# Feed-forward gradients: du and dg of tiles 2 to 14 transposed by DMA, products two tiles behind

## The chip, the cores and the metric

The kernel runs on one core of a Trainium2 chip. The metric is the device time of the whole program, in microseconds. A core has a matrix engine (PE, with its weight loads shown as PEld), a vector engine (DVE), a scalar engine (ACT), GpSimd (POOL) and a queue engine (SP, its DMA issues shown as SPq). 16 DMA engines move data between HBM and the on-chip memory SBUF. Matrix results land in PSUM, which has banks of 128 x 512 f32.

## What is computed

The reference runs a four-layer network forward and then takes the gradients of its input and of all its weights. Layers 0 and 2 are linear attention, layers 1 and 3 are a gated feed-forward block; two sets of weights are shared by the layers of a kind.

```python
def _B_ref(x, w_gate, w_up, w_down):
    g = jnp.einsum("bsd,df->bsf", x, w_gate)
    u = jnp.einsum("bsd,df->bsf", x, w_up)
    h = _sigmoid(g) * u
    return jnp.einsum("bsf,fd->bsd", h, w_down)

x = A_x
x = x + _A_ref(_layernorm(x, axis=-1), A_wqkv, A_wo)
x = x + _B_ref(_layernorm(x, axis=-1), B_w_gate, B_w_up, B_w_down)
x = x + _A_ref(_layernorm(x, axis=-1), A_wqkv, A_wo)
x = x + _B_ref(_layernorm(x, axis=-1), B_w_gate, B_w_up, B_w_down)
...
_out, _vjp = jax.vjp(_f, A_x, A_wqkv, A_wo, B_w_gate, B_w_up, B_w_down)
_grads = _vjp(grad_out)
```

There are S = 2048 rows, D = 512 model columns and F = 1376 feed-forward columns, all bf16 outside. For a feed-forward layer with incoming gradient G the backward pass needs dh = G w_down^T, then du = dh * sigmoid(g) and dg = dh * u * sigmoid(g) * (1 - sigmoid(g)), then the gradient of the normalised input, du w_up^T + dg w_gate^T, the layer norm's own backward step, and the weight gradients, which are products over all rows.

## The kernel before

The rows are 16 tiles of 128 (NST = 16). F is cut into NFC = 11 chunks of 128, the last of 96 columns, and into three slices of 512, 512 and 352 (FSL). The program runs forward through the four layers, then backward through layers 3, 2, 1 and 0. The backward pass of a feed-forward layer is `b_bwd_p1`, called once for layer 3 and once for layer 1; its weight gradients are computed later, from what it stores, in between the next layers' work (`p2_gen`).

The order of instructions on PE, ACT, DVE and POOL is the order in which the code is written (`tc.manual_schedule`). DMA issues, all of them on SP in this kernel, are ordered by a scheduler. A tile of a pool has as many buffers as `bufs` says; an instruction that writes a tile again waits until all that read the old contents in that buffer have ended.

For a tile st, `b_bwd_p1` does this:

- `load`: `ssd`, the two saved factors for du and dg (128 x 2 x 1376, L1101), is loaded from HBM one tile ahead, two buffers; `h_ld` (L1027) comes for two tiles at a time.
- `dhh_mm` (L1004): for each of the three slices, 4 matmuls of `gT` (the transposed gradient tile) with `wdT` into a bank of `dhh_ps`, of which there are two.
- `dd_ops` (L1012): two DVE multiplications for each slice make `dd[:, 0]` (du) and `dd[:, 1]` (dg), bf16. `dd` has two buffers; in layer 3 (`first`) the even tiles use one in the pool `pre` (`pre_dd`), the odd ones another.
- `transposes` (L1079 on PE, L1081 and L1083 on ACT): 22 transposes for each tile, 8, 8 and 6 of them for the three slices, through PSUM (`T_ps`), copied by ACT into `ddT`.
- `store` (L1124, L1126): three DMAs write `dd` to HBM, in pieces of 256 columns (512 bytes) and of 96 columns.
- `dh_mm` (L1113): 22 matmuls of `ddT` with `wuT` and `wgT` into the one bank of `dh_ps`, for the tile before (st-1), in pieces of 11, 5 and 6 between the other work.
- `ln_begin` (`t_sb`, L970 on ACT), `sums` (L975) and `add` (L982, L983) on DVE: the layer norm's backward step, one tile later still.
- `g_tile` and `gT_make`: the incoming gradient of tile st+2 is loaded (layer 3, L1058) or cast and stored (layer 1, L1061 and L1063), and that of st+1 is transposed by 4 PE transposes (L996) and an ACT copy (L997).

So PE's order in iteration st is: 8 matmuls of `dhh` (slices 0 and 1), 11 products of tile st-1, 8 transposes, 4 matmuls of `dhh` (slice 2), 4 transposes of g, 5 products, 8 transposes, 6 products, 6 transposes. After the loop come the 22 products of tile 15.

In layer 3, `mid` loads the eight operand blocks (512 KB each) of the coming weight gradients (`b_operands`, issued at L1202, tiles `p_a`), all after the load of `ssd` for tile 8. In layer 1 the operands are loaded as their buffers come free.

Of the kernel before, what the change touches and what calls it, by code (L numbers as in the profile page):

```python
# [9 lines left out]
BF16 = mybir.dt.bfloat16  # L10
# [8 lines left out]
D = 512  # L19
# [5 lines left out]
NDC = D // P  # L25
NFC = (F + P - 1) // P
FLAST = F - (NFC - 1) * P
FSL = [(0, 512), (512, 512), (1024, F - 1024)]
EPS_LN = 1e-5
EPS = 1e-6  # L30
# [30 lines left out]
def kernel(  # L61
# [78 lines left out]
    with tc.tile_pool(name="wfwd", bufs=1, reuse_waits="tile") as wfwd, ExitStack() as lctx, tc.manual_schedule(engines=EM):  # L140
# [51 lines left out]
        with tc.tile_pool(name="aq2", bufs=1, reuse_waits="tile") as aq:  # L192
            A = kq_fwd(k, aq, 2, lns[2], lns[3])
            hctx.close()
            wb = bctx.enter_context(tc.tile_pool(name="wbwd", bufs=1, side="right", reuse_waits="tile"))
            ocur = {}
            prectx = ExitStack()
            pre = prectx.enter_context(tc.tile_pool(name="pre", bufs=1, side="right", reuse_waits="tile"))
            k.pre = {"pool": pre}

            def out_cb(st):
                if st == NB:
                    k.pre["g"] = pre.tile([P, 2, D], BF16, name="pre_g")
                    nc.sync.dma_start(out=k.pre["g"][:], in_=dram_batch(g_in, 0, 2))
                    k.pre["ssd"] = pre.tile([P, 2, F], BF16, name="pre_ssd")
                    nc.sync.dma_start(out=k.pre["ssd"][:], in_=k.sv[3]["ssd"][rows(0), :, :])
                if st % 2 == 0:
                    ocur["t"] = k.ostg.tile([P, 2, D], BF16, name="out0_t", bufs=2)
                if st >= NST - 2:
                    nc.gpsimd.tensor_scalar(ocur["t"][:, st % 2, :], k.xs[st][:], 1.0, 0.0, ALU.mult, ALU.add)  # L210
                else:
                    nc.scalar.copy(ocur["t"][:, st % 2, :], k.xs[st][:])  # L212
                if st % 2 == 1:
                    nc.sync.dma_start(out=dram_batch(out0, st // 2, 2), in_=ocur["t"][:])

            def last_cb(i):
                if i == 0:
                    k.pre["gT"] = pre.tile([P, NDC, P], BF16, name="pre_gT")
                    g_transposes(k, k.pre["g"][:, 0, :], k.pre["gT"])
                else:  # L220
                    k.pre["dd"] = pre.tile([P, 2, F], BF16, name="pre_dd")
                    for fs in range(2):
                        dd_ops(k, k.pre["dd"], k.pre["ssd"], fs, dhh_mm(k, k.pre["gT"], fs))
            fill = Fill(wT_groups_b(k, wb))
            A.tail(fill)
            ab_fwd(k, A, lns[3], fill, out_cb=out_cb, last_cb=last_cb)
# [5 lines left out]
    if True:  # L232
# [33 lines left out]
                    nc.sync.dma_start(out=dram_batch(out1, st // 2, 2), in_=o1cur["t"][:])  # L266
            return out1_cb

        ops3 = []
        b_bwd_p1(k, 3, lambda: ops3.extend(b_operands(k, R, 3)))  # L270
        prectx.close()
        w3 = p2_gen(k, R, b_jobs(k, 3), False, *ops3)
        next(w3)
# [20 lines left out]
def build_consts(k, consts):  # L294
    nc = k.nc
    neghalf = consts.tile([P, 1], F32, name="neghalf")
    nc.gpsimd.memset(neghalf[:], -0.5)
    ident = consts.tile([P, P], BF16, name="ident")
    nc.gpsimd.memset(ident[:], 0.0)
    nc.gpsimd.affine_select(out=ident[:], in_=ident[:], compare_op=ALU.not_equal, fill=1.0,  # L300
                            base=0, pattern=[[-1, P]], channel_multiplier=1)
    bdmask = consts.tile([P, P], F32, name="bdmask")
    nc.gpsimd.memset(bdmask[:], 1.0)
    nc.gpsimd.affine_select(out=bdmask[:], in_=bdmask[:], compare_op=ALU.is_ge, fill=0.0,
                            base=0, pattern=[[-16, 8], [0, 16]], channel_multiplier=1)
    nc.gpsimd.affine_select(out=bdmask[:], in_=bdmask[:], compare_op=ALU.is_ge, fill=0.0,
                            base=15, pattern=[[16, 8], [0, 16]], channel_multiplier=-1)
    hsmask = consts.tile([P, 8], F32, name="hsmask")
    nc.gpsimd.memset(hsmask[:], 1.0)
    nc.gpsimd.affine_select(out=hsmask[:], in_=hsmask[:], compare_op=ALU.is_ge, fill=0.0,  # L310
                            base=0, pattern=[[-16, 8]], channel_multiplier=1)
    nc.gpsimd.affine_select(out=hsmask[:], in_=hsmask[:], compare_op=ALU.is_ge, fill=0.0,
                            base=15, pattern=[[16, 8]], channel_multiplier=-1)
    e0 = consts.tile([P, P], BF16, name="e0")
    nc.gpsimd.memset(e0[:], 0.0)
    nc.gpsimd.memset(e0[0:1, :], 1.0)
    k.e0 = e0
    k.tab = consts.tile([P, 1], F32, name="tab")
    k.neg = neghalf
    k.ones_sq = consts.tile([P, P], BF16, name="ones_sq")  # L320
    nc.gpsimd.memset(k.ones_sq[:], 1.0)
    k.ident, k.bdmask, k.hsmask, k.neghalf = ident, bdmask, hsmask, neghalf
# [25 lines left out]
def dram_batch(ap2d, b, nb=NB):  # L348
    return ap2d[batch_rows(b, nb), :].rearrange("(n p) d -> p n d", p=P)
# [684 lines left out]
def b_bwd_p1(k, l, mid=None):  # L1034
# [5 lines left out]
    with ExitStack() as ctx:  # L1040
# [41 lines left out]
            if nfull < len(fcs):  # L1082
                nc.scalar.copy(ddT[0:FLAST, :, NFC - 1, :], tps[0:FLAST, :, nfull, :])  # L1083

        def halved(st, nm, pool):
            if not first:
                return pool.tile([P, 2, F], BF16, name=nm)
            if st % 2:
                return pool.tile([P, 2, F], BF16, name=nm, bufs=1)
            if st == 0:  # L1090
                return k.pre[nm]
            return k.pre["pool"].tile([P, 2, F], BF16, name=f"pre_{nm}")

        LD = {}

        def load(st):
            if st >= NST:
                return
            ssd = halved(st, "ssd", ld)
            if not (first and st == 0):  # L1100
                ins = nc.sync.dma_start(out=ssd[:], in_=sv["ssd"][rows(st), :, :])  # L1101
                if mid is not None and st == 8:
                    with tc.issue_after(ins.ins):
                        mid()
            LD[st] = (ssd, hld.get(st))

        def dh_mm(T, lo, hi):
            if lo == 0:
                T["dh"] = ps_tile(k, "y", [P, D], F32, "dh_ps")
            for i in range(lo, hi):  # L1110
                a, fc = divmod(i, NFC)
                r = fc_rows(fc)
                nc.tensor.matmul(T["dh"][:], lhsT=T["ddT"][0:r, a, fc, :], rhs=(k.wuT, k.wgT)[a][0:r, fc, :],  # L1113
                                 start=(i == 0), stop=(i == 2 * NFC - 1))
# [6 lines left out]
        def store(T):  # L1121
            st, dd = T["st"], T["dd"]
            for a in range(2):
                nc.sync.dma_start(out=sv["hdd"][1 + a, :, :, st, :].rearrange("g p w -> p g w"),  # L1124
                                  in_=dd[:, a, 0:NG * GW].rearrange("p (g w) -> p g w", g=NG))
            nc.sync.dma_start(out=sv["hdl"][1:3, :, st, :].rearrange("a p w -> p a w"), in_=dd[:, :, NG * GW:F])  # L1126

        def last_transposes(T):
            transposes(T, 2)
            store(T)  # L1130

        for st in range(2):
            g_tile(st)
# [1 line left out]
            gTs[0] = k.pre["gT"]  # L1135
        else:
            gT_make(0)
        p1 = p2 = None
        load(0)
        for st in range(NST):  # L1140
            load(st + 1)
            ssd, h_st = LD.pop(st)
            T = dict(st=st, h=h_st, ssd=ssd, dd=halved(st, "dd", wide))
            T["ddT"] = wide.tile([P, 2, NFC, P], BF16, name="ddT")
            for fs in range(2):
                if not (first and st == 0):
                    dd_ops(k, T["dd"], T["ssd"], fs, dhh_mm(k, gTs[st], fs))
                if st == 1 and fs == 0:
                    last_transposes(p1)
            if p2 is not None:  # L1150
                p2["ln"].sums()
            if p1 is not None:
                dh_mm(p1, 0, NFC)
                transposes(T, 0)
            ps = dhh_mm(k, gTs.pop(st), 2)
            dd_ops(k, T["dd"], T["ssd"], 2, ps)
            g_tile(st + 2)
            gT_make(st + 1)
            if p1 is None:
                transposes(T, 0)  # L1160
            else:
                dh_mm(p1, NFC, NFC + 5)
            if p2 is not None:
                p2["ln"].add()
            transposes(T, 1)
            if p1 is not None:
                dh_mm(p1, NFC + 5, 2 * NFC)
                ln_begin(p1)
                last_transposes(T)
            p1, p2 = T, p1  # L1170
        p2["ln"].sums()
        dh_mm(p1, 0, 2 * NFC)
        p2["ln"].add()
        ln_begin(p1)
        p1["ln"].sums()
        p1["ln"].add()


class P2Res:
# [60 lines left out]
def b_operands(k, R, l):  # L1240
    return (p2_load_all(k, R, k.sv[l]["h"], R.pfx + "_a1"), p2_load_all(k, R, k.sv[l]["gbf"], R.pfx + "_a2"))
# [369 lines left out]
```

## Time and profile before

| | us |
|---|---|
| median of 3 runs | 1243.02 |
| range of these runs | 1242.3 to 1243.65 |
| span of the profiled execution | 1244.3 |
| PE busy in it | 1197.8 (96%) |
| DVE busy | 726.8 (58%) |
| ACT busy | 600.7 (48%) |
| POOL busy | 258.1 (21%) |
| DMA | 256.08 MB, mean 206 GB/s |

The profile is of one execution. A window of it gives, for each engine, busy time and number of instructions in that stretch, then the granted clock of PE as a share of full speed, the mean busy share of the 16 DMA engines and what they moved. The DMA share can go over 1, because a packet's time runs from its start to its end and packets overlap. A row of the timeline has start, time over which the merged instructions ran, engine, line, operation, output<-input, count, and in brackets the idle time before and what ended it. A row of waits says which instruction waited for which: time in total, times, longest. SPq rows are the time that SP takes to issue a DMA, not the transfer.

### The profile page before, as it was taken

The numbers are of one execution on the slowest core, as the hardware profiler recorded it, in microseconds if no ns is written. First come the engines' busy times: TensorE is split into PE (matmuls) and PEld (weight loads), VectorE is DVE, ScalarE is ACT, GpSimd is POOL, SyncE is SP. The second block draws the span as 40 slices with busy tenths as digits, with TensorE's granted clock in tenths as the row PEclk, the third lists the DMA queues.
The fourth block names the chain that finished last, engine by engine and source line by source line (L and its number), as shares of the span: only waits on it lengthen the run. The fifth ranks groups of instructions, "written<-read, shape, count | busy, mean of one in ns | idle before, by whom it ended". The sixth has DMA issues, their size and how long they took to land. (4 is left out here: it accounts for less than half of the span.)

```text
span 1244.3 us, 22419 instructions
## 1 busy us (share of the span) xinstructions
PE 1197.8 (96%) x8646; PEld 720.2 (58%) x8646; DVE 726.8 (58%) x1410; ACT 600.7 (48%) x1105; POOL 258.1 (21%) x467
## 2 busy tenths in 40 slices
PE   8989999998999999998989999999999979999998
PEld 4445555455555555554745567755555745567777
DVE  6778886777777456664956620056664956642211
ACT  5677777557676644444626621144545616610001
POOL 4246765105665300000100010000000101200000
PEclk8999999999999999998999999999999989999999
DMA  7934455435536877858644488687767666579774
GB/s 234 300 111 166 167 182 175 167 118 182 198 137 212 280 231 240 265 168 287 227 130 144 126 287 287 175 281 216 215 201 236 172 213 182 162 245 335 238 195 147
DMA packets 266203, 256.08 MB, mean 206 GB/s; under 512 B 43248, under 2 KB 250992, under 8 KB 261232
## 3 DMA queue, kind: packets, MB, share of 16 engines
q1 hardware_dynamic: 266096, 254.65, 64.4%
q8 instruction: 67, 1.10, 0.4%
q14 instruction: 40, 0.33, 0.1%
HBM read 135.69 MB, written 118.92 MB: 205 GB/s over the span
## 5 line engine op out<-in xcount | busy, mean ns | idle before, releaser
L1309 PE MATMUL p_ps<-p_set,p_a 128*128 128x256 bf16 (+1 forms) x1792 | 186.3, 263 | 0.0
L1012 DVE TENSOR_TENSOR dd<-dhh_ps,ssd 128x512 bf16<-128x512 f32 x144 | 82.6, 629 | 157.1 <-PE dhh_ps L1004 150.6
L1309 PEld LDWEIGHTS <-p_a 128*128 128x128 bf16 x1792 | 159.0, 98 | 18.8
L1081 ACT COPY ddT<-T_ps 128x1024 bf16<-128x1024 bf16 (+1 forms) x96 | 82.9, 868 | 126.2 <-PE T_ps L1079 126.2
L866 POOL TENSOR_TENSOR ssd_t<-hh_t,oms 128x512 bf16<-128x512 bf16 (+1 forms) x96 | 101.6, 1064 | 55.0 <-ACT out_t L212 40.9
L1113 PEld LDWEIGHTS <-ddT 128*128 128x128 bf16 (+1 forms) x704 | 66.4, 98 | 70.1 <-issue 1.4
L860 PEld LDWEIGHTS <-hT 128*128 128x128 bf16 x768 | 71.6, 98 | 58.8 <-issue 1.7
L978 POOL TENSOR_SCALAR ab<-c 128x2 f32<-128x2 f32 x64 | 12.3, 192 | 448.8 <-DVE junk L975 437.5
L1288 DVE TENSOR_TENSOR dw_stg<-p_ps,dw_stg 128x512 bf16<-128x512 f32 (+2 forms) x43 | 28.3, 660 | 112.0 <-PE p_ps L1309 78.3
L860 PE MATMUL g_ps<-wg,hT 128*128 128x512 bf16 (+1 forms) x384 | 90.9, 359 | 1.2 <-DVE hT L337 1.2
L860 PE MATMUL u_ps<-wu,hT 128*128 128x512 bf16 (+1 forms) x384 | 90.9, 359 | 0.0
L865 DVE TENSOR_TENSOR hh_t<-u_ps,ssd_t 128x512 bf16<-128x512 f32 (+1 forms) x96 | 61.0, 636 | 48.3 <-PE u_ps L860 28.4
L1004 PE MATMUL dhh_ps<-wdT,gT 128*128 128x512 bf16 x372 | 83.8, 362 | 2.7 <-ACT gT L997 2.7
L1113 PE MATMUL dh_ps<-wgT,ddT 128*128 128x512 bf16 (+1 forms) x352 | 86.2, 379 | 0.0
L1113 PE MATMUL dh_ps<-wuT,ddT 128*128 128x512 bf16 (+1 forms) x352 | 81.3, 379 | 1.2 <-ACT t_sb L970 1.2
L886 PE MATMUL y_ps<-wd,hhT 128*128 128x512 bf16 (+1 forms) x352 | 81.3, 379 | 0.6 <-DVE x L888 0.6
L1297 PE MATMUL p_ps<-p_a,p_set 128*128 128x512 bf16 (+1 forms) x352 | 81.6, 383 | 0.0
L862 ACT ACTIVATE ssd_t<-g_ps 128x512 bf16<-128x512 f32 (+1 forms) x96 | 53.2, 554 | 32.8 <-PE g_ps L860 32.6
L975 DVE SCALAR_TENSOR_TENSOR junk<-t_sb,h_ld 128x512 bf16<-128x512 f32 x64 | 44.0, 687 | 39.8 <-ACT t_sb L970 39.8
L970 ACT ACTIVATE t_sb<-dh_ps,rstd_all 128x512 f32<-128x512 f32 x64 | 44.0, 687 | 38.1 <-issue 20.3
L1568 ACT CAST fin_o<-sg_ps 128x512 bf16<-128x512 f32 x4 | 2.3, 586 | 122.1 <-PE sg_ps L1566 122.1
L1290 ACT CAST dw_stg<-p_ps 128x512 bf16<-128x512 f32 (+2 forms) x43 | 24.0, 561 | 76.5 <-PE p_ps L1309 48.4
(226 smaller groups left out, 2224.2 us busy)
## 6 DMA issues: line engine op xcount, KB each, us to landing
p_set<-sv_hdd SPq DMA_DIRECT2D x30, 1024.0 KB, 6.4
sv_ssd<-ssd_t SPq DMA_DIRECT2D x32, 688.0 KB, 3.4
ssd<-sv_ssd SPq DMA_DIRECT2D x24, 688.0 KB, 5.0
sv_hdd<-dd SPq DMA_DIRECT2D x48, 320.0 KB, 3.5
sv_hdd<-hh_t SPq DMA_DIRECT2D x32, 320.0 KB, 2.6
h_ld<-sv_h SPq DMA_DIRECT2D x32, 256.0 KB, 4.4
p_set<-sv_dqk SPq DMA_DIRECT2D x8, 1024.0 KB, 5.8
p_a<-sv_h SPq DMA_DIRECT2D x12, 512.0 KB, 6.2
```

The lines of the kernel that those rows point to most:

```text
L860: nc.tensor.matmul(ps[:, 0:w], lhsT=hT[:, kc, :], rhs=w_sb[:, kc, c0:c0 + w], start=(kc == 0), stop=(kc == NDC - 1))
L862: nc.scalar.activation(ssd_t[:, 0, c0:c0 + w], g_ps[:, 0:w], ACT.Sigmoid)
L865: nc.vector.tensor_tensor(hh_t[:, c0:c0 + w], u_ps[:, 0:w], ssd_t[:, 0, c0:c0 + w], ALU.mult)
L866: nc.gpsimd.tensor_tensor(ssd_t[:, 1, c0:c0 + w], hh_t[:, c0:c0 + w], oms[:, 0:w], ALU.mult)
L886: nc.tensor.matmul(y_ps[:], lhsT=T["hhT"][0:r, fc, :], rhs=k.wd[0:r, fc, :], start=(fc == 0), stop=(fc == NFC - 1))
L970: k.nc.scalar.activation(self.t[:], dh_ps, ACT.Identity, scale=rstd_col, accum_out=self.c12[:, 0:1])
L1004: k.nc.tensor.matmul(ps[:, 0:w], lhsT=gT[:, jc, :], rhs=k.wdT[:, jc, c0:c0 + w], start=(jc == 0), stop=(jc == NDC - 1))
L1012: k.nc.vector.tensor_tensor(dd[:, a, c0:c0 + w], ps[:, 0:w], ssd[:, a, c0:c0 + w], ALU.mult)
L1081: nc.scalar.copy(ddT[:, :, fcs[0]:fcs[0] + nfull, :], tps[:, :, 0:nfull, :])
L1113: nc.tensor.matmul(T["dh"][:], lhsT=T["ddT"][0:r, a, fc, :], rhs=(k.wuT, k.wgT)[a][0:r, fc, :], start=(i == 0), stop=(i == 2 * NFC - 1))
L1297: nc.tensor.matmul(ps[0:r, :], lhsT=set_t[:, st, j * P:j * P + r], rhs=g_all[:, st, :], start=(st == 0), stop=(st == NST - 1))
L1309: nc.tensor.matmul(ps[:, icl * w:(icl + 1) * w], lhsT=h_all[:, st, ic * P:(ic + 1) * P], rhs=set_t[:, st, 0:w], start=(st == 0), stop=(st ...
```

## The change

The transposes of `dd` for tiles 2 to 14 (`by_dma`) are one DMA each, issued by SP, from all 22 chunks of `dd` to `ddT`. For this `dd` is padded from 1376 to 1408 columns (FP), and POOL writes zeros into the padding of these tiles. `ddT` gets three buffers in place of two. The products of tile st-2 run in iteration st from st = 4 on; those of tiles 0 and 1 run in iterations 1 and 2, iteration 3 has none, and those of tiles 14 and 15 run after the loop. The stores of `dd` are issued by ACT, for tile st-1 in iteration st behind the copy of `gT`. Tiles 0, 1 and 15 keep the PE transposes. In layer 3 the eight operand blocks are loaded one for each iteration from st = 6 on. The constant `bdmask` becomes bf16.

```diff
+FP = NFC * P
...
-        ops3 = []
-        b_bwd_p1(k, 3, lambda: ops3.extend(b_operands(k, R, 3)))
+        ops3, lds3 = [], []
+
+        def mid3(st):
+            if st == 6:
+                for src, nm in ((k.sv[3]["h"], "p2_a1"), (k.sv[3]["gbf"], "p2_a2")):
+                    t = R.big.tile([P, NST, D], BF16, name=nm)
+                    ops3.append(t)
+                    lds3.extend((t[:, b * NB:(b + 1) * NB, :], dram_batch(src, b)) for b in range(NST // NB))
+            if st >= 6 and lds3:
+                o, i = lds3.pop(0)
+                nc.sync.dma_start(out=o, in_=i)
+        b_bwd_p1(k, 3, mid3)
...
-    bdmask = consts.tile([P, P], F32, name="bdmask")
+    bdmask = consts.tile([P, P], BF16, name="bdmask")
...
+        def by_dma(st):
+            return 2 <= st < NST - 1
+
+        def dd_tiles(T):
+            T["dd"] = halved(T["st"], "dd", wide, FP)
+            T["ddT"] = wide.tile([P, 2, NFC, P], BF16, name="ddT", bufs=3)
+            if by_dma(T["st"]):
+                nc.gpsimd.memset(T["dd"][:, :, F:FP], 0.0)
+
+        def dma_T(T):
+            nc.sync.dma_start(out=T["ddT"][:].rearrange("p a c t -> p (a c) t"),
+                              in_=T["dd"][:].rearrange("p a f -> p (a f)"), transpose=True)
...
-                if mid is not None and st == 8:
+                if mid is not None:
                     with tc.issue_after(ins.ins):
-                        mid()
+                        mid(st)
...
             for a in range(2):
-                nc.sync.dma_start(out=sv["hdd"][1 + a, :, :, st, :].rearrange("g p w -> p g w"),
-                                  in_=dd[:, a, 0:NG * GW].rearrange("p (g w) -> p g w", g=NG))
-            nc.sync.dma_start(out=sv["hdl"][1:3, :, st, :].rearrange("a p w -> p a w"), in_=dd[:, :, NG * GW:F])
+                nc.scalar.dma_start(out=sv["hdd"][1 + a, :, :, st, :].rearrange("g p w -> p g w"),
+                                    in_=dd[:, a, 0:NG * GW].rearrange("p (g w) -> p g w", g=NG))
+            nc.scalar.dma_start(out=sv["hdl"][1:3, :, st, :].rearrange("a p w -> p a w"), in_=dd[:, :, NG * GW:F])
...
+            p1 = Ts[st - 1] if st else None
+            p = p1 if st in (1, 2) else Ts[st - 2] if st >= 4 else None
+            q = done[-1] if done and not done[-1].get("end") else None
...
-            if p2 is not None:
-                p2["ln"].sums()
-            if p1 is not None:
-                dh_mm(p1, 0, NFC)
+            if q is not None:
+                q["ln"].sums()
+            if p is not None:
+                dh_mm(p, 0, NFC)
+            if not by_dma(st):
                 transposes(T, 0)
             ps = dhh_mm(k, gTs.pop(st), 2)
             dd_ops(k, T["dd"], T["ssd"], 2, ps)
             g_tile(st + 2)
             gT_make(st + 1)
...
+            if p1 is not None:
+                store(p1)
+            if by_dma(st):
+                dma_T(T)
+            if p is not None:
+                dh_mm(p, NFC, NFC + 5)
...
+        store(T)
+        for p in Ts[NST - 2:]:
+            q = done[-1]
+            q["ln"].sums()
+            dh_mm(p, 0, 2 * NFC)
+            q["ln"].add()
+            ln_begin(p)
+            done.append(p)
```

More of the change, by code (lines that the diff above doesn't have):

```diff
@@ L220, in last_cb @@
                 else:
-                    k.pre["dd"] = pre.tile([P, 2, F], BF16, name="pre_dd")
+                    k.pre["dd"] = pre.tile([P, 2, FP], BF16, name="pre_dd")
                     for fs in range(2):
@@ L1083, in transposes, with halved @@
                 nc.scalar.copy(ddT[0:FLAST, :, NFC - 1, :], tps[0:FLAST, :, nfull, :])
-        def halved(st, nm, pool):
+        def halved(st, nm, pool, w=F):
             if not first:
-                return pool.tile([P, 2, F], BF16, name=nm)
+                return pool.tile([P, 2, w], BF16, name=nm)
             if st % 2:
-                return pool.tile([P, 2, F], BF16, name=nm, bufs=1)
+                return pool.tile([P, 2, w], BF16, name=nm, bufs=1)
             if st == 0:
                 return k.pre[nm]
-            return k.pre["pool"].tile([P, 2, F], BF16, name=f"pre_{nm}")
+            return k.pre["pool"].tile([P, 2, w], BF16, name=f"pre_{nm}")
+        def by_dma(st):
[8 more added lines that the diff above has]
+                              in_=T["dd"][:].rearrange("p a f -> p (a f)"), transpose=True)
         LD = {}
@@ L1123, in store @@
             for a in range(2):
-                nc.sync.dma_start(out=sv["hdd"][1 + a, :, :, st, :].rearrange("g p w -> p g w"),
-                                  in_=dd[:, a, 0:NG * GW].rearrange("p (g w) -> p g w", g=NG))
[L1126 to L1130, printed above, removed]
+                nc.scalar.dma_start(out=sv["hdd"][1 + a, :, :, st, :].rearrange("g p w -> p g w"),
+                                    in_=dd[:, a, 0:NG * GW].rearrange("p (g w) -> p g w", g=NG))
+            nc.scalar.dma_start(out=sv["hdl"][1:3, :, st, :].rearrange("a p w -> p a w"), in_=dd[:, :, NG * GW:F])
         for st in range(2):
@@ L1137, in b_bwd_p1 @@
             gT_make(0)
-        p1 = p2 = None
         load(0)
+        Ts, done = [], []
         for st in range(NST):
@@ L1142, in b_bwd_p1 @@
             ssd, h_st = LD.pop(st)
-            T = dict(st=st, h=h_st, ssd=ssd, dd=halved(st, "dd", wide))
-            T["ddT"] = wide.tile([P, 2, NFC, P], BF16, name="ddT")
+            T = dict(st=st, h=h_st, ssd=ssd)
+            dd_tiles(T)
+            p1 = Ts[st - 1] if st else None
+            p = p1 if st in (1, 2) else Ts[st - 2] if st >= 4 else None
+            q = done[-1] if done and not done[-1].get("end") else None
             for fs in range(2):
@@ L1148, in b_bwd_p1 @@
                 if st == 1 and fs == 0:
-                    last_transposes(p1)
-            if p2 is not None:
-                p2["ln"].sums()
-            if p1 is not None:
-                dh_mm(p1, 0, NFC)
+                    transposes(p1, 2)
+            if q is not None:
[3 more added lines that the diff above has]
+            if not by_dma(st):
                 transposes(T, 0)
@@ L1158, in b_bwd_p1 @@
             gT_make(st + 1)
[L1159 to L1165, printed above, removed]
-            if p1 is not None:
[L1167 to L1176, printed above, removed]
+            if p1 is not None:
+                store(p1)
[3 more added lines that the diff above has]
+                dh_mm(p, NFC, NFC + 5)
+            if q is not None:
+                q["ln"].add()
+                q["end"] = True
+            if not by_dma(st):
+                transposes(T, 1)
+            if p is not None:
+                dh_mm(p, NFC + 5, 2 * NFC)
+                ln_begin(p)
+                done.append(p)
+            if st and not by_dma(st):
+                transposes(T, 2)
+            Ts.append(T)
+        store(T)
[3 more added lines that the diff above has]
+            dh_mm(p, 0, 2 * NFC)
+            q["ln"].add()
+            ln_begin(p)
+            done.append(p)
+        p["ln"].sums()
+        p["ln"].add()
 class P2Res:
```

## The prediction

> **What bounds the kernel now.** The change works inside two stages, the feed-forward backward passes of layers 3 and 1 (`b_bwd_p1`), so I asked first for the windows of these stages. They run from 434.0 to 570.6 us and from 812.0 to 948.6 us, 136.6 us each, 273.2 us of a span of 1244.3 us.
>
> ```profile
> core 0: us, PE busy (x) PEld busy (x) DVE busy (x) ACT busy (x) POOL busy (x), PEclk, DMA share, GB/s
> 434.00:570.60 136.60, 134.51 (x945) 74.81 (x942) 83.02 (x153) 63.24 (x110) 4.02 (x17) 1.00 0.73 226
> 812.00:948.60 136.60, 135.83 (x951) 75.65 (x949) 85.09 (x156) 63.24 (x110) 10.30 (x28) 1.00 0.74 224
> ...
> 881.40:883.60 2.20, 2.20 (x21) 1.33 (x19) 1.03 (x2) 1.45 (x2) 0.00 (x0) 1.00 0.96 268
> 884.40:886.00 1.60, 1.60 (x9) 0.71 (x8) 1.60 (x3) 0.29 (x2) 0.00 (x0) 1.00 0.88 289
> 492.00:506.00 14.00, 14.00 (x99) 7.66 (x96) 7.70 (x14) 7.39 (x14) 0.19 (x1) 1.00 1.10 346
> ```
>
> TensorE is busy 98 and 99% of both stages at the full granted clock; DVE 62%, ACT 46%. The 16 DMA engines are next: share 0.73 and 0.74. The last three windows are a stretch of `dd` stores alone, one of an `ssd` load alone, and the burst of operand loads in layer 3.
>
> Then the timeline of one tile in layer 1, and the waits of PE there.
>
> ```profile
> 880.07 0.96 DVE L1012 TENSOR_TENSOR dd<-dhh_ps,ssd 128x352 bf16<-128x352 f32 x2 [1.20 <-PE dhh_ps L1004]
> ...
> 880.62 0.93 SPq L1124 DMA_DIRECT2D sv_hdd<-dd  x2
> ...
> 881.60 0.66 SPq L1126 DMA_DIRECT2D sv_hdl<-dd  x1
> ...
> 882.31 0.99 SPq L1101 DMA_DIRECT2D ssd<-sv_ssd  x1
> ...
> 884.98 2.54 PE L1113 MATMUL dh_ps<-wuT,ddT 128*128 128x512 bf16 x11
> ...
> 887.36 0.61 PE L1079 MATMUL T_ps<-ident,dd 128*128 128x128 bf16 x8
> ...
> 889.15 0.36 SPq L1124 DMA_DIRECT2D sv_hdd<-dd  x1
> ```
>
> ```profile
> PE dh_ps L1113 <- ACT t_sb L970: 0.6, 1, 0.6
> ```
>
> A tile's first store is issued at 880.62 and the next tile's at 889.15: the period is 8.53 us, and PE waits 0.6 us for others in the whole stage. A transpose costs PE (0.61 - 0.219) / 7 = 0.056 us (0.219 is the duration of a single one in the row of `T_ps`), a product (2.54 - 0.379) / 10 = 0.216 us. So the 22 transposes of a tile are 1.23 us of the 8.53.
>
> **The change part by part.** *Removed from PE:* 22 transposes in 13 tiles of two layers, 26 x 1.23 = 32 us. All of it is on the path now. PE alone would need 136.6 - 16.0 = 120.6 us for each stage, 7.30 us for a tile.
>
> *Removed from ACT:* four copies in each such tile, 2 x 1.01 + 0.58 + 0.37 = 2.97 us, worth nothing: ACT is idle half the time and waits for PE.
>
> *Stores moved to ACT.* ACT gets three issues a tile, 0.93 + 0.66 = 1.6 us by SP's rows, less than the copies it loses. Behind them in ACT's queue stands `t_sb` (L970), which frees the only bank of `dh_ps`; the next product comes 8 matmuls, 1.7 us, later, so an issue may be some 1.7 us late before PE feels it. The stores of tile st are now issued in iteration st+1, after the copy of `gT`, not in iteration st. `dd` has two buffers, so tile st+2 may not write before they have landed. That makes a loop of one period: the first pair of `dd` 1.36, the third `dhh_ps` up to the `gT` transposes 0.6 and these 0.4, wait and copy of `gT` 0.8, two issues 0.93, landing of the third store 3.2 (the issues' row for `sv_hdl`): 7.3 us. It is hidden by PE's 7.30 only just, and reaches the old period at a landing of 4.4 us; the landings of `dd` stores went from 2.6 to 8.2 us. The landing depends on the load of the rings, next.
>
> *Added: 26 DMAs that transpose.* Each reads 128 x 2816 bf16, 720,896 bytes, and writes as much, SBUF to SBUF. No row of the trace has one; it lies on the same 16 DMA engines as everything else if it is like the DMAs seen. Bounds on its DMA time T: moved like the `ssd` load (289 GB/s at a share of 0.88, so 328 at 1.0) it is 2.2 us; like the stores in 512-byte pieces (268 at 0.96, so 279) 2.6 us. In the packet records of 872 to 889 us a packet of 192 bytes takes 16 ns, one of 512 bytes 28 ns; a block row of 128 bf16 is 256 bytes, some 18.5 ns between the two, and 2816 of them over 16 engines make 3.2 us. [...] I take 3.2 us, the row of the piece that the source really has. A DMA time below nothing is excluded: no transfer is taken away.
>
> [...]
>
> *Its DMA time against the stage.* Layer 3: 0.73 x 136.6 = 99.7 us now, plus 13 x 3.2 = 41.6, is 141.3 us. Layer 1: 101.1 + 41.6 = 142.7 us. I take a share of 1.0 as full, since stores alone and `ssd` alone ran at 0.96 and 0.88 while they had the rings; the burst of plain loads showed 1.10. So the rings, not PE, would end both stages: +4.7 and +6.1 us against 136.6.
>
> *SP's queue.* The built program has one transposing instruction for each tile, which waits for the third pair of `dd`, and behind it the `ssd` load of the second next tile and, every other tile, `h_ld` and the g load or store. Before, three stores (1.6 us) stood there. Bounds for its issue: 0.36 us, the shortest issue seen, to 22 of these, 7.9 us, if each 128 x 128 block is issued by itself. I take 1.0 us, the `ssd` load's, as it is one instruction; then SP's turn gets shorter and nothing is late.
>
> *Products two tiles behind.* A transpose asked for at mid iteration st is used 8 matmuls into iteration st+2, some 11 us later at a period of 8.5; that hides 1.0 of issue, 3.2 of DMA and 2 of latency. Iteration 3 has no product, so there the cover is thin: what is left of iteration 2 (2.4 us), 3.7 us of `dd` work, 1.7 us. I put 2 us a layer for this fill and for rings idle at the ends, bounds 0 and 5 us. After the loop two products run instead of one; the work is the same.
>
> *Loads spread, mask, padding.* Eight operand loads of layer 3 go one to a tile instead of all after tile 8. The old burst cost PE 1.33 us (the window 489.1 to 515.0 has 24.57 busy of 25.90); that 1.33 is inside the stage that the ring bound replaces, so it isn't counted twice. 26 memsets of 128 x 64 on POOL, at most 0.6 us each by the cast of `gstage` (L1061), with POOL busy 4 and 10 us in a stage: hidden. `bdmask` in bf16: two multiplications in all, nothing.
>
> Sum: +4.7 + 6.1 + 2 + 2 = +14.8 us, 1259.1 against the profiled 1244.3. The runs' median, 1243.02, is 1.3 below that execution, so **1258 us**.
>
> **The rivals.**
>
> *The transposes are cheap, faster.* Place: the DMA rings. If T is under (136.6 - 99.7 - 2) / 13 = 2.7 us, or the rings take the mix at the 1.10 of the burst, the rings have room and PE's 32 us come out in part. At T = 2.2 the stages need 128.3 and 129.7 us: -8.3 - 6.9 + 4 = -11, 1232. At most PE's bound, -32 + 4: 1215. For it: the burst kept 346 GB/s with PE at 100%. Against it: two fifths of a tile's DMA time go to 512-byte pieces, and the store loop has no slack.
>
> [...]
>
> *SP's issue grows with the blocks.* At 7.9 us, SP needs 7.9 + 1.0 + 0.4 + 0.4 = 9.7 us a tile against 8.53: 26 x 1.2 + 4 = +35, 1278. It decides from an issue of 6.7 us, and earlier in part, since `ssd` then lands late. For it: no issue seen covers a transpose. Against: two stores of 640 pieces each took 0.93 together, so issues don't grow with pieces.
>
> [...]
>
> **How the numbers follow.** Forecast, rings or store loop at about the old period or a little over: 0.42, own range 1242 to 1275. Cheap transposes: 0.33. SP's issue: 0.13. Small pieces: 0.12. Range 1222 to 1312: below lies the best third of the cheap case, above most of the small pieces, some 0.19 in all. The runs spread over 0.11%, so 0.2% (2.5 us) is what can be told from no change. Faster: 0.33. Same: 0.06, from the forecast's lower edge. Slower: 0.36 + 0.13 + 0.12 = 0.61.
>
> **What would show it.** In the profile after: DMA share of both stages near 1.0, GB/s above 280, PE busy some 121 of about 142 us, with idle ended by `dd` (L1023 in the new numbering) or by `ddT`; DVE's `dd` waiting for a store; landings of `sv_hdd` over 4.4 us. A share clearly under 0.9 with a longer stage would refute the ring bound and point to SP's issue or latency; SP's own rows give the issue. Stages under 134 us, with PE busy over 90%, make the prediction wrong on the faster side.

## The result: 1293.9 us, four per cent slower

The changed kernel took 1293.94 us (median of 3 runs, 1292.15 to 1294.83) against 1243.02 us: a ratio of 1.040, 95% interval 1.0374 to 1.0425. The profiled execution has a span of 1292.2 us, 47.9 more than before. The direction held, the size did not: 51 us where 15 were forecast. The time lies above the forecast's own range (1242 to 1275) and inside the whole range, which leaves room for the rivals.

The windows of the two stages after, from the same first work to the end of the last products (columns as before the change):

```profile
core 0: us, PE busy (x) PEld busy (x) DVE busy (x) ACT busy (x) POOL busy (x), PEclk, DMA share, GB/s
434.00:597.40 163.40, 133.24 (x648) 62.29 (x645) 81.82 (x152) 28.11 (x58) 5.60 (x30) 0.92 1.01 257
831.60:998.00 166.40, 134.81 (x664) 63.97 (x662) 83.65 (x155) 28.68 (x58) 12.23 (x41) 0.90 0.96 240
```

They grew from 136.6 us each to 163.4 and 166.4. PE is idle for 30 and 32 us of them, the DMA share went from 0.73 and 0.74 to 1.01 and 0.96, and the granted clock fell to 0.92 and 0.90. PE has fewer matmuls: 664 records in the second stage, 951 before. But its busy time hardly shrank (133.2 and 134.8 us, before 134.5 and 135.8); the section on the prediction comes back to this. The two stages grew by 56.6 us and the whole by 47.9, so some 9 us come back in the rest of the program.

What DVE waited for in the two stages (line; what ended the wait: total us, times, longest), and the rows of `ddT`: durations of SP's issue as least, median and most, and the landing of the transposes:

```profile
DVE dd L1023 <- DMA sv_hdl<-dd: 34.0, 6, 7.5
DVE pre_dd L1023 <- DMA sv_hdl<-pre_dd: 33.0, 7, 7.1
...
DVE dd L1023 <- DMA sv_hdl<-dd: 70.1, 14, 8.8
...
L1115 SPq DMA_TRANSPOSE ddT<-dd x19: 4588/5596/8936, 460.0 to 970.5; - x19
L1115 SPq DMA_TRANSPOSE ddT<-pre_dd x7: 4452/5761/7007, 452.7 to 571.1; - x7
...
DMA to landing us min/median/max: 6.3/7.9/10.9
```

137 us of waits of `dd` end with the landing of a store, `sv_hdl`, the last of a tile's three. None ends with the landing of a transposing DMA. Issuing a transpose takes SP 4.5 to 8.9 us. A tile in layer 1, in the timeline:

```profile
868.89 0.39 PE L1007 MATMUL gT_ps<-ident,gstage 128*128 128x128 bf16 x4
...
869.45 0.99 ACTq L1148 DMA_DIRECT2D sv_hdd<-dd  x2
869.79 0.32 SPq L1125 DMA_DIRECT2D ssd<-sv_ssd  x1
...
870.48 0.91 ACTq L1150 DMA_DIRECT2D sv_hdl<-dd  x1
870.78 7.96 SPq L1115 DMA_TRANSPOSE ddT<-dd  x1
...
878.92 2.48 DVE L1023 TENSOR_TENSOR dd<-dhh_ps,ssd 128x512 bf16<-128x512 f32 x4 [8.62 <-DMA sv_hdl<-dd]
...
880.27 1.33 PE L1015 MATMUL dhh_ps<-wdT,gT 128*128 128x352 bf16 x4 [4.50 <-DVE dd L1023]
```

The last store is issued at 870.48 and the `dd` that waits for it starts at 878.92, 8.4 us later, where the prediction put 3.2. This is one of the longest; the median from issue to landing of `sv_hdl` in this run is 5.9. DVE waits 8.62 us, and PE after it 4.50.

So there were two suspects: the loop through two `dd` buffers and late stores (theory A), or rings that are simply full (theory B, the forecast).

### The profile page after: what moved, and what is told of

Read it like the earlier page. It is cut to its first block, busy times and chain, and to the rows that moved or that the text cites. A ratio compares the mean times of both kernels' runs of the same rounds, so it can differ in the third digit from the quotient of the medians.

```text
span 1292.2 us, 21349 instructions
## 1 busy us (share of the span) xinstructions
PE 1192.5 (92%) x8074; PEld 696.1 (54%) x8074; DVE 724.7 (56%) x1410; ACT 531.3 (41%) x1001; POOL 261.8 (20%) x493
## 5 line engine op out<-in xcount | busy, mean ns | idle before, releaser
L1015 PE MATMUL dhh_ps<-wdT,gT 128*128 128x512 bf16 x372 | 88.3, 375 | 52.5 <-DVE dd L1023 33.3
L1137 PEld LDWEIGHTS <-ddT 128*128 128x128 bf16 (+1 forms) x704 | 72.8, 105 | 92.5 <-issue 27.3
L1137 PE MATMUL dh_ps<-wgT,ddT 128*128 128x512 bf16 (+1 forms) x352 | 100.7, 443 | 0.0
L1015 PEld LDWEIGHTS <-gT 128*128 128x128 bf16 x372 | 36.8, 101 | 96.3 <-issue 56.4
L1008 ACT COPY gT<-gT_ps 128x512 bf16<-128x512 bf16 x31 | 18.2, 586 | 160.4 <-PE gT_ps L1007 160.4
L986 DVE SCALAR_TENSOR_TENSOR junk<-t_sb,h_ld 128x512 bf16<-128x512 f32 x64 | 44.0, 687 | 47.9 <-ACT t_sb L981 47.9
```

The lines of the kernel that those rows point to most:

```text
L986: nc.vector.scalar_tensor_tensor(junk[:], self.t[:], 1.0, self.h, ALU.mult, ALU.mult, accum_out=self.c12[:, 1:2])
L1015: k.nc.tensor.matmul(ps[:, 0:w], lhsT=gT[:, jc, :], rhs=k.wdT[:, jc, c0:c0 + w], start=(jc == 0), stop=(jc == NDC - 1))
```

## The experiments

Ratios are against the kernel before, run beside each on the same chip; 0.01 is 12.4 us. The changed kernel itself has 1.040.

**A third buffer for `dd`.** Room for it in layer 3 comes from `gstage` (three buffers, not four) and the scratch of `sums` (one, not two).

```diff
-            T["dd"] = halved(T["st"], "dd", wide, FP)
...
+            if not first:
+                T["dd"] = wide.tile([P, 2, FP], BF16, name="dd", bufs=3)
...
+            elif st % 3 == 0:
+                T["dd"] = k.pre["pool"].tile([P, 2, FP], BF16, name="pre_dd")
+            else:
+                T["dd"] = wide.tile([P, 2, FP], BF16, name="dd", bufs=2)
```

> The changed kernel with a third buffer for dd (in layer 3 gstage has three buffers in place of four and the scratch of sums one in place of two, to make room). Theory A, the reuse loop: the stores of dd are issued one tile late and crawl beside the transposes, and with two buffers the next dd waits for them (137 us of waits of dd for sv_hdl in the two stages). With a third buffer these waits go and the period falls from about 10.2 us to that of SP's queue (5.6 + 0.5 + 0.4 + 0.4 = 7 us) or of the rings (about 9): 1255 to 1275. Theory B, the rings are full (share 1.01 and 0.96 of the stages), and the wait for a store is only where that shows: 1288 to 1296, with the wait moved to ssd or ddT.

Measured: 1274.6 us, 1.0268 (1.0251 to 1.0285). The waits for stores are no longer among the long ones, and 42 us of waits of `dd` for `ssd` have come. The loop cost something, but more than half of the loss is still there. Some of that may be the price of the room: PE now waits 14.6 us in all for loads of `gstage`, which gave up a buffer.

**Prompt stores, by ACT and by SP.** In the first, ACT issues the stores of a tile at the end of its own iteration. In the second, SP does, ahead of the tile's transpose; this is its edit.

```diff
-            if p1 is not None:
+            if st == 1:
                 store(p1)
+            if by_dma(st):
+                store(T)
             if by_dma(st):
                 dma_T(T)
...
-                nc.scalar.dma_start(out=sv["hdd"][1 + a, :, :, st, :].rearrange("g p w -> p g w"),
+                nc.sync.dma_start(out=sv["hdd"][1 + a, :, :, st, :].rearrange("g p w -> p g w"),
```

> The changed kernel with the stores of a tile issued by ACT at the end of its own iteration, half a period earlier. Theory A: the reuse loop gets about 3 us more room, 1260 to 1280. Theory B, full rings: 1288 to 1298, no gain.

> The changed kernel with the stores back on SP, ahead of the tile's transpose, so that one queue serves stores, then transpose, then ssd, in order. Theory A: stores land about 3.3 us after their issue as before the change, the loop is gone, SP has 1.6 + 5.6 + 0.5 + 0.4 + 0.4 = 8.5 us a tile: 1255 to 1275. Theory B: the bytes are the same, 1288 to 1298; above 1300 if SP's issue time is the bound.

Measured: 1271.2 us, 1.0227 (1.0200 to 1.0254), and 1264.6 us, 1.0183 (1.0166 to 1.0199). Issuing the stores in their own tile wins back some 22 us, and giving them to SP another 5. 23 us remain with almost no wait for a store (4.5 us, once). The stages of the second one, and the waits of DVE over both:

```profile
433.30:583.00 149.70, 124.18 (x625) 57.00 (x623) 80.15 (x149) 25.50 (x53) 5.30 (x29) 0.97 1.06 273
823.70:964.60 140.90, 121.09 (x625) 57.38 (x623) 80.08 (x149) 25.48 (x53) 12.29 (x41) 0.98 1.08 271
```

```profile
DVE dd L1023 <- DMA ssd<-sv_ssd: 73.7, 18, 6.0
...
DVE pre_dd L1023 <- DMA pre_ssd<-sv_ssd: 27.4, 6, 5.9
```

The rings have a share of 1.06 and 1.08 from end to end, and the load that is last in the queue, `ssd`, is what is waited for. The packet records say more than the share: between 465 and 545 us and between 850 and 930 us, the time in which no packet is in flight is 0.3%; in the kernel before it is 17 and 15%.

**All transposes on PE, the rest as changed.**

```diff
         def by_dma(st):
-            return 2 <= st < NST - 1
+            return False
```

> The changed kernel with no tile transposed by DMA: products two tiles behind, stores by ACT one tile late, loads spread, but all transposes on PE. Both theories: the loop is 7.3 us with a store landing of 3.2, and the rings have a share of 0.73, so PE's 8.53 us a tile hide both: 1241 to 1249. Rival C, that the lag and the late stores by ACT alone cost much of the 51 us: above 1260.

Measured: 1294.9 us, 1.0448 (1.0404 to 1.0492). Both theories were wrong here: without a single transposing DMA the kernel is as slow as with 26 of them. The second stage and the waits of DVE:

```profile
838.90:1000.40 161.50, 141.36 (x911) 74.88 (x909) 80.63 (x149) 60.01 (x105) 10.33 (x28) 0.96 0.60 179
```

```profile
DVE dd L1023 <- DMA sv_hdl<-dd: 76.2, 16, 8.9
DVE pre_dd L1023 <- DMA sv_hdl<-pre_dd: 36.4, 7, 6.4
```

The rings are only 60% used, with no packet in flight for 30 and 38% of the same two stretches, yet `dd` waits 113 us for stores. A loop, not a lack of room. The timeline of one turn of it in layer 3:

```profile
498.75 2.48 DVE L1023 TENSOR_TENSOR dd<-dhh_ps,ssd 128x512 bf16<-128x512 f32 x4 [6.62 <-DMA sv_hdl<-dd]
...
500.33 0.76 PE L1015 MATMUL dhh_ps<-wdT,gT 128*128 128x352 bf16 x4
...
501.49 0.37 ACTq L1148 DMA_DIRECT2D sv_hdd<-pre_dd  x1
...
502.47 0.81 ACTq L1150 DMA_DIRECT2D sv_hdl<-pre_dd  x1
...
502.74 0.33 SPq L1125 DMA_DIRECT2D ssd<-sv_ssd  x1
503.12 1.29 SPq L280 DMA_DIRECT2D p_a<-sv_h  x1
...
508.98 2.48 DVE L1023 TENSOR_TENSOR pre_dd<-dhh_ps,pre_ssd 128x512 bf16<-128x512 f32 x4 [4.82 <-DMA sv_hdl<-pre_dd]
```

From `dd` to `dd` 10.23 us: 1.58 to the third `dhh_ps`, 2.14 to the issue of the last store, 6.51 from there to the next `dd`. The first two terms are close to the prediction's (3.7 in place of 4.1); the third was put at 3.2.

The landing is the term that moved. These rows give it for `sv_hdl` (least, median, most): first the kernel before and the version below with lag and loads alone, both with prompt stores on SP, then this run and the kernel before with late stores by ACT, none of the four with a transposing DMA.

```profile
DMA to landing us min/median/max: 2.6/3.3/7.4
DMA to landing us min/median/max: 3.0/3.5/7.7
DMA to landing us min/median/max: 3.0/5.8/8.3
DMA to landing us min/median/max: 3.1/5.6/10.4
```

Why a store on ACT's ring needs longer can be seen in the packet records of this run in layer 1. Packets started in each 0.5 us, stores (512 bytes, ACT's ring) beside `ssd` (5504 bytes, SP's ring):

```
us      stores  ssd
868.5     290     0
871.5      88    21
872.0      22    26
872.5      23    34
873.0      38    31
```

Alone, 290 store packets start in 0.5 us. Beside `ssd`, about one for each `ssd` packet, which is eleven times as large and takes 211 ns (median), a store packet 27 to 29. On one ring the stores went first and `ssd` after them: in the kernel before, the 1536 store packets of the tile that the prediction's timeline shows start from 881.5 to 884.2 us, the 128 of `ssd` from 884.1 to 886.8.

**The kernel before, with late stores by ACT alone.**

```diff
             gT_make(st + 1)
+            if p1 is not None:
+                store(p1)
```

(with `nc.scalar` in `store`, and the store at the end of the iteration taken out; the last tile's comes after the loop)

> The kernel before, with one thing changed: the three stores of dd are issued by ACT, one tile late, behind the copy of gT. Theory A, reuse loop: the period of the two stages goes to about 10.2 us as in the run with all transposes on PE, 1285 to 1295. If the loop needs the lag or the spread loads as well: 1245 to 1260.

Measured: 1280.7 us, 1.0299 (1.0261 to 1.0337), a little under the span expected, with the wait expected:

```profile
DVE dd L1012 <- DMA sv_hdl<-dd: 87.8, 21, 10.1
DVE pre_dd L1012 <- DMA sv_hdl<-pre_dd: 39.5, 7, 8.9
```

This edit by itself costs 37 us. It changes two things at once, when the stores are issued and by whom; late stores on SP's queue were not tried.

**Lag of two and spread loads alone.** Stores prompt by SP, transposes all on PE.

> The kernel with the stores back on SP in their own tile (run e3_store_sp, 1264.6 us) with all transposes on PE again: what is left of the change is the lag of two tiles, the spread loads and the padding. If the lateness of the stores made the 51 us of the run without DMA transposes, this is as before: 1239 to 1247. If the lag of two tiles itself costs (its two products after the loop, its empty iteration 3), 1250 or more.

Measured: 1240.9 us, 0.9993 (0.9969 to 1.0018). No change to be told, as expected.

**`ssd` ahead of the transpose, or off SP, or everything relieved.** Three edits on the version with prompt stores by SP (1264.6 us): the transpose issued behind the next `ssd` load; the `ssd` loads issued by ACT; and that together with a third `dd` buffer.

```diff
             load(st + 1)
+            if st and by_dma(st - 1):
+                dma_T(Ts[st - 1])
```

```diff
-                ins = nc.sync.dma_start(out=ssd[:], in_=sv["ssd"][rows(st), :, :])
+                ins = nc.scalar.dma_start(out=ssd[:], in_=sv["ssd"][rows(st), :, :])
```

> Run e3_store_sp with the transpose of a tile issued by SP behind the next load of ssd in place of ahead of it. If the 23 us that are left there come from ssd standing behind the transpose (101 us of waits of dd for ssd): 1240 to 1255, the waits gone. If the rings are full and only the bytes count: 1260 to 1268, with the wait moved to ddT or to a store.

> Run e3_store_sp (1264.6 us) with the ssd loads issued by ACT, so that SP has stores and transposes alone, 1.6 + 5.6 = 7.2 us a tile and no load waits behind a transpose's issue. If SP's queue is what the 23 us over before come from: 1243 to 1255. If the bytes on the rings are: 1258 to 1268.

> Run g2_ssd_act with a third buffer for dd as well: full transposes by DMA, prompt stores, no load behind a transpose, no reuse of dd within two tiles. Queues and buffers are then no reason any more. If only the time on the rings is left as a bound (6.2 + 3.2 = 9.4 us a tile against 8.53): 1255 to 1266. If it was queues and buffers: 1215 to 1245.

Measured: 1266.0 us, 1.0193 (1.0164 to 1.0222); 1280.4 us, 1.0293 (1.0256 to 1.0331); 1275.4 us, 1.0248 (1.0196 to 1.0300). The first only moved the wait: 86 us of `dd` for the reader of its buffer, the transpose, and 41 us of PE for `ddT`. The second made it worse: with the loads on ACT's ring, single landings of `ssd` reach 19.2 us (8.5 before) and of a transpose 21.9 (9.2 with all on SP). That fits the sharing of two rings seen above, but wasn't tried by itself. The third stayed above its span, with a share of 1.10 and 1.06:

```profile
434.00:584.00 150.00, 121.92 (x612) 56.96 (x611) 80.24 (x147) 25.29 (x52) 4.99 (x29) 0.91 1.10 269
822.00:966.00 144.00, 120.35 (x626) 57.83 (x627) 83.54 (x152) 27.97 (x55) 11.85 (x39) 0.93 1.06 268
```

No order of queues or spare buffer that was tried brings 13 full transposes a layer under the old time. What they have in common is the pace. From the `dd` of tile 3 to that of tile 14 in layer 1, a tile takes on average 9.02 us with the third buffer and late stores, 9.00 and 8.99 with prompt stores by ACT and by SP, 8.98 with `ssd` first and 9.03 with everything relieved; only `ssd` by ACT alone differs, at 9.69. With everything relieved about half of the turns take 7.3 us, PE's own time by the prediction, and every few tiles one takes 13 to 14: spare buffers move the wait, and the average stays. Full rings fit this, as the bytes are the same in all five.

SP's queue is not ruled out in the same way. In the middle of these stages SP is issuing for 94% of the time with prompt stores by SP, 94 to 95% with `ssd` first and still 90 to 91% with `ssd` by ACT, so none of these edits freed it. Against it as the bound: what it issues differs between the five versions while the pace doesn't, and the issue of a transpose stretches, from a median of 5.0 us in the middle of layer 1 with prompt stores by SP to 7.1 with stores by ACT. `ssd` first together with a third buffer, all on SP's ring, was not tried with full transposes.

**Half the bytes.** du alone by DMA; the 11 transposes of dg and their copies stay on PE and ACT; stores prompt by SP.

```diff
-            nc.sync.dma_start(out=T["ddT"][:].rearrange("p a c t -> p (a c) t"),
-                              in_=T["dd"][:].rearrange("p a f -> p (a f)"), transpose=True)
+            nc.sync.dma_start(out=T["ddT"][:, 0], in_=T["dd"][:, 0, :], transpose=True)
```

> Run e3_store_sp with du alone transposed by DMA (11 blocks, half the bytes) and dg by PE. If the rings' time counts, half of it, 1.6 us, goes, and PE, with 11 transposes a tile, needs 7.9 us: 1230 to 1245. If a fixed cost of each transposing DMA counts (its issue, its place in the queue): 1252 to 1264.

Measured: 1236.2 us, 0.9944 (0.9921 to 0.9967): faster than both kernels. Its stages:

```profile
435.00:569.00 134.00, 125.96 (x769) 65.04 (x767) 80.95 (x149) 46.40 (x106) 4.98 (x29) 0.99 1.01 270
813.00:941.20 128.20, 124.47 (x770) 64.60 (x768) 81.08 (x150) 46.58 (x106) 12.15 (x41) 1.00 1.01 262
```

PE is at 94 and 97% again. Against the version with the lag alone, whose stages are 133.9 us each, the gain is all in layer 1; in layer 3 the rings were the fuller ones already, with a share of 0.78 against 0.73 in layer 1. Half the blocks also shorten SP's issue (medians of 4.9 and 4.8 us with prompt stores by SP, 3.2 and 3.7 here), so this run doesn't part the two.

**On top of it:** a third `dd` buffer with the transpose behind `ssd`; or `ssd` by ACT.

> Run f4_du_only (du alone by DMA, stores prompt on SP, 1236.2 us) with a third buffer for dd (room made as in e1_third_dd) and the transpose issued behind the next ssd load. If the waits of dd for ssd (45 us) are what keeps f4 from PE's 7.9 us a tile: 1222 to 1233. If its rings are full already: 1234 to 1240.

> Run f4_du_only with the ssd loads issued by ACT. If SP's queue holds f4 back: 1222 to 1233. If not: 1234 to 1242; above that if a load with 5.5 KB packets on a second ring slows the stores as it did in the changed kernel.

Measured: 1235.1 us, 0.9932 (0.9909 to 0.9956), not told apart from the run without; and 1245.7 us, 1.0026 (0.9999 to 1.0053): with loads on a second ring the gain is lost.

## Why the prediction was wrong in size

*The step that failed is the landing in the store loop.* The prediction wrote the loop down term by term, named the point from which it decides (a landing of 4.4 us), and then put the landing at 3.2, the median of stores that had SP's ring in order before them. On ACT's ring, beside `ssd`, it is 5.6 and 5.8 (medians of `sv_hdl` in the two runs with PE transposes and late stores), and with PE transposes the loop turns in 10.5 and 10.1 us on average (layers 3 and 1), not 7.3. "It is hidden by PE's 7.30 only just" should have read: it decides. The edit alone costs 37 us; on top of the transposes prompt stores are worth 27 (1.0400 to 1.0183). The prediction expected the landing to depend on the load of the rings, and that holds too: with prompt stores by SP and the transposes on the same ring the median is 5.8, but then the stores are issued a whole tile earlier.

*The ring bound was right and a little small.* With the loop out of the way, the version with prompt stores by SP is at +23 us, where the forecast had +14.8. Three terms were off. The first is the transposes' time. Their packets of 256 bytes have a median of 18 ns, as expected (18.5), but in that version a mean of 22.4, so 3.9 us a transpose and not 3.2, 9 us more for each stage. The second goes the other way: the rings took a share of 1.06 and 1.08, not 1.0. From its first to its last `dhh` the stages grew by 11.3 and 3.1 us, 14.4 in all, against 10.8 forecast. The third is the end of the stage. The fill was put at 4 in all, and the two products after the loop at nothing, on the ground that "the work is the same". That holds only while PE is the bound: the run with the lag alone has the same longer tail (14.4 us from the last `dhh` to the last product, 8.5 before) and loses nothing in all, since its loop, with one product less in it, is shorter: from the first to the last `dhh` its stages take 127.9 and 128.2 us, before 132.3 and 129.7. With full rings PE idles in the loop and the tail comes on top: 5.9 us a stage, 11.8 in all. Loop and tail make 26.2 us. The span of this profiled execution grew by only 15.2, as the parts ahead of, between and behind the two stages are 4.3, 5.3 and 1.3 us shorter in it; why is open.

*PE's 32 us* mostly did not come out, not even as busy time. From the first to the last product of a stage PE was busy for 131.5 and 131.1 us before, 130.6 and 129.7 in the changed kernel, and 124.2 and 121.1 with prompt stores by SP, where 16 less were forecast. The clock goes with it: in the changed kernel it was granted at half for 27 and 31 us of these two stretches, with prompt stores by SP for 10 and 7, before never. *ACT* had room: it is busy for 28.1 and 28.7 us of the two stages. *SP's issue* was mis-sized, 5.6 us in place of 1.0. In the changed kernel SP is issuing for 73 and 69% of the middle of the stages (465 to 560 and 860 to 960 us), so it is not the bound there; in the 23 us that are left with prompt stores, its part and the rings' are not told apart.

*Rivals.* Cheap transposes: not so. 3.9 us is over the 2.7 from which it would decide. Its other condition, rings that take the mix at 1.10, nearly came about, but even so a tile needs (6.2 + 3.9) / 1.10 = 9.2 us, against 8.53. The run with half of each, 2.4 us of ring time by its packets, is the case that this rival described, and it is faster. The 328 GB/s of the 2.2 us with which the rival was worked out did not come: with prompt stores by SP at most 572 of its packets start in 0.5 us, 293 GB/s, and from the first to the last packet it takes 3.6 us in the median, 200 GB/s. Small pieces, which the chances count with 0.12: no run shows them. The 13 transposes of a stage are 36,608 packets of 256 bytes in the changed kernel, 2816 for each. SP's issue: 5.6 us, short of the 6.7 from which it would decide.

*The sign to look for* was given rightly ("DVE's `dd` waiting for a store; landings of `sv_hdd` over 4.4 us"; their median in the changed kernel is 5.0), but the two ways had one chance and one sum. That the time still lies in the whole range is luck: the room above 1275 was kept for SP's issue and small pieces, and neither decided. The rates looked for were too high: 257 and 240 GB/s came, not 280.

The difference between late stores with the old lag (1.0299) and with the lag of two (1.0448) is mostly the same tail, 5.9 us a stage, for in both the stage is bound by the loop; the remaining 7 us are longer loops (1.9 and 5.6 us from the first to the last `dhh` in the two profiles), and why they are longer was not tried.

## What to carry to other kernels

Before an engine is relieved, add up what takes over in the stage: here the rings had 27% to spare, and 22 blocks a tile needed 37 to 46% of the old period; 11 blocks, at 28%, just fitted. Where a store frees a buffer that the next tile but one writes, its issue time plus landing is a term of the period (from the issue to the next `dd`, 6.51 of the 10.23 us in the turn above): issue it as soon as its data are there. And don't take a landing from one queue as the price on another: here, without transposing DMAs, the median went from 3.3 us on SP's ring to 5.6 and 5.8 on ACT's, and small packets on the second ring went at the pace of the large packets beside them (22 to 38 in 0.5 us beside 26 to 34, 290 alone).

## What the runs showed of the hardware that was not expected

- One transposing DMA of 128 x 2816 bf16 keeps SP busy for 4.5 to 8.9 us in the changed kernel (median 5.6 and 5.8); with half the columns 1.4 to 4.9 us (median 3.2 and 3.7). The time is not a fixed price: with half the columns and the transpose behind `ssd`, the medians are 1.8 and 2.8.
- Packets of two queues started about one for one: 290 packets of 512 bytes in 0.5 us alone, 22 to 38 beside 26 to 34 packets of 5504 bytes.
- The granted clock of 0.90 to 0.92 is a mean of stretches at full and at half, 3.4 and 6.8 us long, and before the change these two stages have no stretch at half. Two of them in the changed kernel, then the one between:

```profile
850.50:857.20 6.70, 5.61 (x18) 2.44 (x18) 5.12 (x10) 0.58 (x1) 0.77 (x2) 0.50 0.41 105
877.80:884.50 6.70, 4.23 (x15) 2.02 (x15) 5.37 (x10) 0.58 (x1) 0.92 (x3) 0.50 0.93 252
857.30:877.70 20.40, 14.96 (x75) 6.89 (x74) 8.71 (x16) 2.73 (x6) 1.65 (x5) 1.00 1.09 242
```

The second begins in the 4.50 us for which PE waits in the timeline above. What of the 51 us this makes was not tried by itself; the run with all transposes on PE is as slow with 10 and 14 us at half clock.
